# Filling idle TensorE time by a leaky bucket of owed columns instead of a trailing sum, in a transformer layer

## The chip, the cores and the metric

The kernel runs on one core of a Trainium2 chip. A core has five engines that matter here, each with its own instruction queue that it works off in order: TensorE (PE, with its weight loads shown apart as PEld), VectorE (DVE), ScalarE (ACT), GpSimd (POOL) and SyncE (SP), which only starts DMAs. The metric is device time in microseconds (us) from the start of an execution to its end. Three executions of the kernel before took 1261.03, 1268.29 and 1271.53 us, so the median is 1268.29. Such a time is one whole execution; the profile shows one more.

## The reference

One layer on 2048 tokens of width 512, all in bf16: a layer norm without scale, attention with 32 heads of 16, the output projection and a residual; then a second layer norm, a gated feed-forward part (GEGLU, width 1792) and a residual.

```python
qkv = layernorm(x) @ wqkv                      # 512 -> 3 * 512, 32 heads of 16
scores = einsum("bhqd,bhkd->bhqk", q, k) * 16 ** -0.5
o = einsum("bhqk,bhkd->bhqd", softmax(scores), v)
h = x + merge_heads(o) @ wo
n = layernorm(h)
out = h + (gelu(n @ w_gate) * (n @ w_up)) @ w_down
```

The scores are 32 x 2048 x 2048, and every one goes through an exponential on ACT. That is the largest piece of work.

## The kernel before, in words

**Tiles and units.** The queries are cut into four chunks of 512 (`c`), the heads into eight groups of four (`slot`). A unit is one chunk and one slot, 32 units in all. In a unit, `qk` goes over 16 key tiles of 128 and four heads: one tile is a matmul of 32 rows of the array (a head's 16 values beside another's, which the query mask sets to zero) with 512 query columns, into a PSUM bank of 128 x 512. Four such matmuls with different rows of the array can run side by side. `exps` takes the exponential of three or two banks at a time (the steps, in turn on banks 0 to 2 and 3 to 4; bank numbers are those of `SLOTS`) into the ring `PT`. `pv` multiplies four tiles of `PT` with the values: 17 columns a head (16 values and a column of ones for the softmax sum), four heads side by side in strips of the array's columns, summed over the 16 key tiles in bank `PVB`. After the 16th, `ofin` copies that bank out on DVE (L1340), transposes it on PE (L1344) and divides.

**Dense work.** Projections (at the start) and, per chunk, the output projection, the layer norm (`post`) and the feed-forward part (`gates`, `ups`, `downs`) are full-array matmuls into two further banks (`DENSE`, 6 and 7). They are laid into the time in which ACT works on the exponentials. The last chunk's follow behind the attention.

**What sets the order.** The order of every engine is set before the kernel runs, by a planner in Python (`Sched`). Each operation has a guessed duration (`TMM` 0.24 us for a matmul of 512 columns, `TQK` 0.34 for a step's score matmuls, `TPV` 0.33 for a value group, 0.093 + 0.427 us a tile for an exponential), the planner keeps a clock for each engine (`sch.t`) and picks the operation that can start first, with priorities (scores -10, values -5, dense work by due times). On the chip each engine then works its list off in that order and waits on semaphores; the guessed durations play no part any more.

**Fills.** Ahead of each PE operation that the planner is about to issue, `run` calls `fill(st)`, where `st` is the operation's planned start. A fill is a matmul of a 128 x 128 weight of zeros (`zero_bf`) with 512 columns of ones. It adds zero to `PVB` while a unit's sum is under way (L1511), and otherwise writes a free dense bank (L1521). `t0` is the time at which it could start; `st - t0` is the gap. If `fill` issues one, it is called again for the same operation. Each PE operation carries its column count, `cols`: 512 for a fill, 128 for each score matmul (a quarter of the array's rows), 512 for a value group, 512 for each dense matmul. `busy_columns` adds up the columns of the operations that ended in the last 3.4 us of planned time, and `fill` issues nothing where that sum is 3900 or more.

The matmuls of the profile stand under helper lines: L1144 is any dense matmul, L1145 any matmul with a place in the array, so the scores (`pbank<-QT,KT`) and the values (`pbank<-PT,VA`), L1151 any ACT operation made by `ACTF` (the exponentials).

Of the kernel before, what the change touches and what calls it, by code (L numbers as in the profile page):

```python
# [5 lines left out]
class _Eng:  # L6
    def __init__(self, name, sem):
        self.name = name
        self.sem = sem
        self.count = 0  # L10
        self.ops = []
        self.known = {}
        self.group_start = None
# [155 lines left out]
NT, NCH, NSLOT = 16, 4, 8  # L169
# [5 lines left out]
NT, NCH, NSLOT = 16, 4, 8  # L175
# [703 lines left out]
class Sched:  # L879
# [5 lines left out]
    def __init__(self, P, banks):  # L885
        self.P = P
        self.t = {n: 0.0 for n in P.ENGINES}
        self.done = {}
        self.streams = []
        self.banks = [(0.0, b) for b in banks]  # L890
        self.now = 0.0
        self.fill = None
        self.cols = []

    def add(self, gen, prio):
        s = Stream(gen, prio)
# [29 lines left out]
                    r = max(r, self.done[tok])  # L926
        return r + LAT

    def busy_columns(self, t):

        while self.cols and self.cols[0][0] < t - 3.4:
            self.cols.pop(0)
        return sum(n for _, n in self.cols)

    def _emit(self, op, start):
        if op.cols:
            self.cols.append((start + op.dur, op.cols))
        P = self.P
        extra = op.extra() if op.extra else ()
        for tok in extra:  # L940
            start = max(start, self.done[tok] + LAT)
        self.now = max(self.now, start)
        end = start + op.dur
        if op.dma is not None:
            tok = P.dma(op.eng, op.fns[0], op.dma, reads=op.reads, writes=op.writes, extra_deps=extra)
            self.t[op.eng] = start + 0.1
            self.done[tok] = end
        else:
            if op.eng == "pe":
                P.group_begin("pe")  # L950
            n = len(op.fns)
            for i, fn in enumerate(op.fns):
                tok = P.op(op.eng, fn, reads=op.reads, writes=op.writes, sig=(i == n - 1), extra_deps=extra)
            if op.eng == "pe":
                P.group_end("pe")
            self.t[op.eng] = end
            self.done[tok] = end
        if op.then is not None:
            op.then()
# [54 lines left out]
TMM, TTR, TTR32, TQK, TPV = 0.24, 0.12, 0.26, 0.34, 0.33  # L1014
SLOTS = ((0, 3), (3, 2))
PVB = 5
DENSE = (6, 7)
COLS = 3900


def bass_sequential_preLN__mha_block__geglu_ffn__prompt_kernel(nc, A_x, A_wqkv, A_wo, B_x, B_w_gate, B_w_up, B_w_down, out):
# [37 lines left out]
def fast_path(nc, P, base0, ARENA, pbank, flag, A_x, A_wqkv, A_wo, B_x, B_w_gate, B_w_up, B_w_down, out):  # L1059
# [67 lines left out]
    while sum(n for _, n, _ in STEPS) < len(TILES):  # L1127
        b0, n = SLOTS[len(STEPS) % len(SLOTS)]
# [6 lines left out]
    sch = Sched(P, list(DENSE))  # L1135
    C = dict(exp=0, pv=0, oa=0, ln1=0, proj=0, oproj=0, gut=0, down=0, act=0)
# [375 lines left out]

    def fill(st):

        if sch.t["pe"] < 10 or C["down"] >= 4 * NCH - 1:
            return False
        if C["pv"] % NT and C["pv"] < NT * NU:
            op = fill_op
        elif sch.banks:
            b = min(sch.banks)[1]  # L1520
            op = Op("pe", TMM, lambda e: e.matmul(pbank[:, b, :], zero_bf[:], ones_bf[:], start=True, stop=True), reads=["zero_bf", "ones_bf"], writes=[("pb", b)], cols=512)  # L1521
        else:
            return False
        t0 = max(sch.t["pe"], sch._ready(op))
        if st - t0 < TMM or sch.busy_columns(t0) >= COLS:
            return False
        sch._emit(op, t0)
        C["fill"] = C.get("fill", 0) + 1
        return True
# [58 lines left out]
```

## Time and profile before

| | before |
|---|---|
| median of three executions | 1268.29 us (1261.03 to 1271.53) |
| the profiled execution | 1261.9 us |
| its span, first to last instruction | 1260.1 us |
| mean granted TensorE clock | 0.708 |
| PE busy | 1138.9 us (90%), 5723 matmuls |
| ACT busy | 997.6 us (79%) |
| DVE, POOL busy | 259.5 us, 181.7 us |

In the page, the part with 40 slices gives each engine's busy share in tenths for each fortieth of the span (9 is 90% or more), and PEclk the share of full speed that TensorE's clock was granted. A busy PE is not PE at its peak: a matmul takes longer at a lower clock and is busy all that time. The windows view gives the same for stretches that one chooses, with the count of instructions in brackets; PEld counts weight loads, of which each matmul has one. In a row of groups or waits, what stands behind the bar or the arrow is the engine's idle time and what ended it. Some matmul records are missing in the trace: 386 fills of L1511 have a record and 435 of their weight loads.

### The profile page before, as it was taken

How to read it: one execution, taken by the hardware profiler on the slowest of the kernel's cores; microseconds unless marked ns; L12 is line 12 of the kernel's file. 1: busy time of each engine (PE TensorE's matmuls, PEld its weight loads, DVE VectorE, ACT ScalarE, POOL GpSimd, SP SyncE). 2: the span in 40 equal slices, each digit the busy share in tenths (PEclk: the TensorE clock that was granted, in tenths of full speed). 3: DMA queues.
4: the chain of work that ended last, by engine and by line, in shares of the span. 5: the costliest groups of instructions: out<-in, count | busy, mean ns of one | idle time of the engine just before them, and what ended most of it. 6: DMA issues, size and time to landing. Idle time of an engine off the chain costs nothing.

```text
span 1260.1 us, 14333 instructions
## 1 busy us (share of the span) xinstructions
PE 1138.9 (90%) x5723; PEld 276.7 (22%) x5827; DVE 259.5 (21%) x462; ACT 997.6 (79%) x897; POOL 181.7 (14%) x191
## 2 busy tenths in 40 slices
PE   7899999988998979989999999899989989999887
PEld 2222111111222221111222211111222221111132
DVE  5336100000355100000345100000056200000052
ACT  3799877777899997878889977777799997787610
POOL 6400000000076000000067000000058100000010
PEclk8899655555699995555689955555599985555599
DMA  4000500000000100000000000000000000000000
GB/s 133 1 1 1 192 1 1 1 1 1 1 2 1 35 1 1 1 1 1 1 1 1 25 10 1 1 1 1 1 1 2 9 26 1 1 1 1 1 1 20
DMA packets 12844, 14.91 MB, mean 12 GB/s; under 512 B 1760, under 2 KB 11744, under 8 KB 12768
## 3 DMA queue, kind: packets, MB, share of 16 engines
q1 hardware_dynamic: 12768, 13.90, 3.4%
q8 instruction: 48, 0.79, 0.3%
q14 instruction: 28, 0.23, 0.1%
HBM read 11.80 MB, written 2.10 MB: 11 GB/s over the span
## 4 chain that ended last, share of the span: by engine, by line
PE 72%; ACT 10%; POOL 7%; issue 6%; DVE 2%; ACTq 0%; DVEq 0%
PE pbank L1145 39%; PE pbank L1511 16%; PE pbank L1144 13%; ACT PT L1151 10%; POOL w_sb L1433 3%; PE pbank L1344 2%; POOL w_sb L1431 2%; POOL w_sb L1432 2%; DVE OA L1340 1%; POOL xn_sb L1220 1%; PE pbank L1521 1%; PE pbank L1381 0%; DVE g_sb L1429 0%; DVE QT L1268 0%; ACT w_sb L1439 0%
## 5 line engine op out<-in xcount | busy, mean ns | idle before, releaser
L1151 ACT ACTIVATE PT<-pbank 128x1536 bf16<-128x1536 f32 (+1 forms) x819 | 959.3, 1247 | 180.6 <-PE pbank L1145 177.0
L1145 PE MATMUL pbank<-QT,KT 32*128 32x512 bf16 x2048 | 420.7, 509 | 44.0 <-ACT PT L1151 39.0
L1145 PE MATMUL pbank<-PT,VA 128*17 128x512 bf16 x2048 | 264.3, 506 | 2.2 <-DVE OA L1340 1.0
L1511 PE MATMUL pbank<-ones_bf,zero_bf 128*128 128x512 bf16 x386 | 226.6, 587 | 36.5 <-PE pbank L1145 21.3
L1145 PEld LDWEIGHTS pbank<-QT,KT 32*128 32x128 bf16 x2048 | 83.3, 95 | 364.4 <-ACT PT L1151 160.7
L1340 DVE COPY OA<-pbank 128x512 f32<-128x512 f32 x32 | 22.1, 690 | 672.4 <-PE pbank L1145 672.4
L1397 POOL TENSOR_SCALAR rstd_95<-mv_94 128x1 f32<-128x1 f32 x16 | 3.6, 223 | 976.6 <-DVE mv_94 L1395 976.6
L1511 PEld LDWEIGHTS pbank<-ones_bf,zero_bf 128*128 128x128 bf16 x435 | 44.7, 103 | 216.4 <-PE pbank L1511 117.5
L1145 PEld LDWEIGHTS pbank<-PT,VA 128*17 128x17 bf16 x2048 | 50.4, 89 | 182.6 <-PE pbank L1511 68.9
L1144 PE MATMUL pbank<-wd_sb,GUT 128*128 128x512 bf16 x211 | 58.6, 382 | 3.2 <-PE pbank L1145 1.3
L1433 POOL TENSOR_TENSOR w_sb<-w_sb,g_sb 128x512 f32<-128x512 f32 x42 | 54.7, 1303 | 3.5
L1431 POOL TENSOR_TENSOR w_sb<-g_sb 128x512 f32<-128x512 f32 x42 | 47.9, 1141 | 31.6 <-DVE g_sb L1429 31.5
L1344 PE MATMUL pbank<-ident_77,OA 128*128 128x128 f32 x128 | 37.6, 388 | 4.5 <-DVE OA L1340 3.6
L1440 DVE SCALAR_TENSOR_TENSOR w_sb<-w_sb,g_sb 128x512 f32<-128x512 f32 x42 | 35.3, 840 | 18.9 <-ACT w_sb L1439 18.6
L1144 PE MATMUL pbank<-xnT,wqkv_sb 128*128 128x512 bf16 x121 | 36.9, 391 | 2.0 <-DVE xnT L1234 0.7
L1429 DVE COPY g_sb<-pbank 128x512 f32<-128x512 f32 x42 | 29.0, 690 | 40.2 <-PE pbank L1144 40.1
L1445 ACT ACTIVATE w_sb<-pbank 128x512 f32<-128x512 f32 x14 | 8.4, 597 | 35.8 <-PE pbank L1144 35.8
L1439 ACT ACTIVATE w_sb<-w_sb 128x512 f32<-128x512 f32 x42 | 26.7, 635 | 8.7 <-POOL w_sb L1433 8.7
L1432 POOL TENSOR_SCALAR w_sb<-w_sb 128x512 f32<-128x512 f32 x42 | 32.9, 784 | 3.7
L1465 DVE SCALAR_TENSOR_TENSOR GUT<-pbank,w_sb 128x512 bf16<-128x512 f32 x42 | 28.7, 688 | 19.7 <-PE pbank L1144 19.3
L1268 DVE TENSOR_SCALAR QT<-pbank,qmask 128x512 bf16<-128x512 f32 x31 | 23.3, 751 | 8.1 <-PE pbank L1144 6.8
L1220 POOL TENSOR_SCALAR xn_sb<-x_sb,mv,rstd 128x512 bf16<-128x512 bf16 x12 | 24.8, 2076 | 0.5 <-issue 0.3
(99 smaller groups left out, 470.9 us busy)
## 6 DMA issues: line engine op xcount, KB each, us to landing
xres<-in_A_x_dram SPq DMA_DIRECT2D x16, 128.0 KB, 3.3
out_dram<-out_sb SPq DMA_DIRECT2D x16, 128.0 KB, 1.7
wg_sb<-in_B_w_gate_dram SPq DMA_DIRECT2D x1, 1792.0 KB, 7.0
wu_sb<-in_B_w_up_dram SPq DMA_DIRECT2D x1, 1792.0 KB, 12.4
wd_sb<-in_B_w_down_dram SPq DMA_DIRECT2D x1, 1792.0 KB, 17.1
x_sb<-in_A_x_dram SPq DMA_DIRECT2D x3, 512.0 KB, 7.8
wqkv_sb<-in_A_wqkv_dram SPq DMA_DIRECT2D x2, 384.0 KB, 8.1
x_sb<-in_A_x_dram SPq DMA_DIRECT2D x2, 256.0 KB, 3.2
```

The costliest lines, as they stand in the source:

```text
L1144: return lambda e: e.matmul(o, l, r, start=start, stop=stop)
L1145: return lambda e: e.matmul(o, l, r, start=start, stop=stop, tile_position=tile)
L1151: return lambda e: e.activation(out=o, in_=i, func=func, **kw)
L1220: lambda e, t=t: e.tensor_scalar(out=xn_sb[:, t % 8, :], in0=x_sb[:, t, :], scalar1=mv[:, t, 0:1], scalar2=rstd[:, t:t + 1], op0=ALU.subtr ...
L1340: yield Op("dve", 0.61, lambda e: e.tensor_copy(out=OA[:, par, :], in_=pbank[:, PVB, :]), reads=[("pb", PVB)], writes=[("OA", par)])
L1344: yield Op("pe", 2 * TTR32, cols=256, fns=[lambda e, qt=qt: e.transpose(out=pbank[:, b, 128 * qt:128 * qt + 128], in_=OA[:, par, 128 * qt: ...
L1429: yield Op("dve", 0.61, lambda e: e.tensor_copy(out=gs, in_=pbank[:, b, :]), reads=[("pb", b)], writes=[("g", i)], extra=dE)
L1431: yield Op("pool", 1.05, lambda e: e.tensor_tensor(out=ws, in0=gs, in1=gs, op=ALU.mult), reads=[("g", i)], writes=[("w", i)])
L1432: yield Op("pool", 0.62, lambda e: e.tensor_scalar(out=ws, in0=ws, scalar1=GA, scalar2=1.0, op0=ALU.mult, op1=ALU.add), reads=[("w", i)], ...
L1433: yield Op("pool", 1.27, lambda e: e.tensor_tensor(out=ws, in0=ws, in1=gs, op=ALU.mult), reads=[("w", i), ("g", i)], writes=[("w", i)])
L1440: yield Op("dve", 0.6, lambda e: e.scalar_tensor_tensor(out=ws, in0=ws, scalar=1.0, in1=gs, op0=ALU.add, op1=ALU.mult), reads=[("w", i), ( ...
L1511: fill_op = Op("pe", TMM, lambda e: e.matmul(pbank[:, PVB, :], zero_bf[:], ones_bf[:], start=False, stop=False, skip_group_check=True), re ...
```

## The change

The trailing sum `busy_columns` goes, and `owed` takes its place: a number of columns that grows by 1250 with each microsecond of planned time, up to 1500, and from which each planned PE operation takes its columns at its planned end, down to zero and no further. A fill is now issued

- if 800 or more are owed, whatever the gap is, also where the gap is negative and the fill starts after the time at which the operation behind it could have;
- if 300 or more are owed and the gap is at least 0.06 us;
- if 100 or more are owed and the gap is at least `TMM`, 0.24 us.

Before, the gap had to be 0.24 us in all cases. The first fill may now come after the first score step is planned, where it was 10 us of PE's planned time. The fill itself, its banks and its end are as they were.

```diff
-        self.cols = []
+        self.debt = (0.0, 0.0)
...
-    def busy_columns(self, t):
-
-        while self.cols and self.cols[0][0] < t - 3.4:
-            self.cols.pop(0)
-        return sum(n for _, n in self.cols)
+    def owed(self, t, n=0):
+
+        d = min(1500.0, self.debt[1] + RATE * (t - self.debt[0]))
+        if n:
+            self.debt = (t, max(0.0, d - n))
+        return d

     def _emit(self, op, start):
         if op.cols:
-            self.cols.append((start + op.dur, op.cols))
+            self.owed(start + op.dur, op.cols)
...
-COLS = 3900
+RATE = 1250
+OWED = (100, 300, 800)
...
-        if sch.t["pe"] < 10 or C["down"] >= 4 * NCH - 1:
+        if "qk" not in C or C["down"] >= 4 * NCH - 1:
             return False
...
         t0 = max(sch.t["pe"], sch._ready(op))
-        if st - t0 < TMM or sch.busy_columns(t0) >= COLS:
+        n, gap = sch.owed(t0), st - t0
+        if n < OWED[0] or (gap < TMM and n < OWED[1]) or (gap < 0.06 and n < OWED[2]):
             return False
```

## The prediction

> **What bounds the kernel now.** I read the page first, for the clock over the span.
>
> ```profile
> span 1260.1 us, 14333 instructions
> ...
> PE   7899999988998979989999999899989989999887
> ...
> ACT  3799877777899997878889977777799997787610
> POOL 6400000000076000000067000000058100000010
> PEclk8899655555699995555689955555599985555599
> ```
>
> One slice is 31.5 us. The granted TensorE clock is full where projections or the feed-forward part run beside the attention, and half in four long stretches where the attention runs alone. PE shows nine tenths in both, so its busy share says nothing about the clock. ACT shows 9 at full clock and 7 at half. POOL's work, the feed-forward part's, starts in the slice after each of the three rises in the middle of the span. The windows view, cut at the changes of the clock, gives the sizes (columns: us, then the busy time and instruction count of PE, PEld, DVE, ACT and POOL, then the granted clock, DMA share, GB/s):
>
> ```profile
> 63.00:133.90 70.90, 67.49 (x444) 18.92 (x448) 37.72 (x56) 69.24 (x61) 0.00 (x0) 1.00 0.05 14
> 133.90:335.30 201.40, 184.53 (x797) 37.98 (x807) 8.84 (x20) 156.04 (x133) 0.00 (x0) 0.50 0.07 26
> 437.70:468.40 30.70, 23.78 (x163) 6.98 (x163) 1.38 (x3) 30.70 (x28) 0.00 (x0) 1.00 0.06 17
> 468.40:618.60 150.20, 138.15 (x599) 28.81 (x609) 6.77 (x15) 117.43 (x100) 0.00 (x0) 0.50 0.00 1
> 724.40:915.50 191.10, 175.80 (x755) 36.16 (x768) 9.29 (x20) 148.39 (x127) 0.00 (x0) 0.50 0.01 2
> 1028.20:1196.00 167.80, 153.12 (x652) 31.16 (x663) 6.19 (x13) 129.24 (x111) 0.00 (x0) 0.50 0.00 1
> 1196.00:1260.10 64.10, 52.92 (x225) 18.57 (x230) 24.57 (x48) 8.36 (x14) 3.16 (x8) 0.95 0.03 10
> ```
>
> At full clock the kernel is bound by ACT: its exponentials are busy 69.24 of 70.90 us (0.977) beside the projections, and 30.70 of 30.70 in the one stretch of attention alone that kept the clock. In the four half-clock stretches, 710.5 us together, ACT works 551.1 us (0.776) and waits for the score matmuls. The waits and the groups put this on the same lines:
>
> ```profile
> ACT PT L1151 <- PE pbank L1145: 177.0, 216, 7.0
> ...
> L1151 ACT ACTIVATE PT<-pbank 128x1536 bf16<-128x1536 f32 (+1 forms) x819 | 959.3, 1247 | 180.6 <-PE pbank L1145 177.0
> ```
>
> So 177 us of ACT's waiting is what is to be won, 159.4 us of it in those stretches (710.5 - 551.1).
>
> **What sets the clock.** The clock's changes lie on a grid of about 3.41 us, so I cut six such windows of attention alone at full clock and counted the weight loads in each (matmul records can be missing, so I count PEld). First line L1145, the scores and the value matmuls (each worth 128 columns of the whole array: 32 of 128 rows, or a 32-wide strip of columns), then L1511, the fills (512 columns each):
>
> ```profile
> 441.07:444.48 3.41, 1.43 (x16) 0.40 (x16) 1.00 0.00 0
> 451.31:454.72 3.41, 1.66 (x18) 0.48 (x15) 1.00 0.00 0
> 461.55:464.96 3.41, 1.26 (x13) 0.29 (x9) 1.00 0.00 0
> 464.96:468.38 3.42, 2.14 (x18) 0.63 (x18) 1.00 0.00 0
> 720.96:724.38 3.42, 1.82 (x15) 0.54 (x15) 1.00 0.32 93
> 1024.75:1028.16 3.41, 2.02 (x18) 0.54 (x15) 1.00 0.00 0
> ...
> 441.07:444.48 3.41, 0.62 (x2) 0.19 (x2) 1.00 0.00 0
> 451.31:454.72 3.41, 1.17 (x3) 0.38 (x4) 1.00 0.00 0
> 461.55:464.96 3.41, 1.07 (x3) 0.38 (x4) 1.00 0.00 0
> 464.96:468.38 3.42, 0.22 (x2) 0.10 (x1) 1.00 0.00 0
> 720.96:724.38 3.42, 0.36 (x1) 0.10 (x1) 1.00 0.32 93
> 1024.75:1028.16 3.41, 0.27 (x1) 0.10 (x1) 1.00 0.00 0
> ```
>
> The first three were followed by full clock: 16 x 128 + 2 x 512 = 3072 columns, 15 x 128 + 4 x 512 = 3968, 9 x 128 + 4 x 512 = 3200. The last three were each followed by the drop: 18 x 128 + 512 = 2816, 15 x 128 + 512 = 2432, and 2432 again. So I read the clock as kept by about 2900 columns in a window, and the fills as counting: without them 451.31 would stand at 1920 and should have dropped.
>
> **The change, part by part.** Before, a fill needed a gap of 0.24 us in the plan (TMM) and fewer than 3900 columns in the last 3.4 us. Now owed columns grow by 1250 per us up to 1500, each planned matmul pays its columns off, and a fill goes in at 800 owed whatever the gap (even ahead of a ready score matmul), at 300 if the gap is at least 0.06 us, and at 100 if it is 0.24. The bucket can't go below zero, so dense work earns no credit and owes again at once when it stops; the old sum went on holding the dense columns for 3.4 us.
>
> *Number of fills.* One pair of steps of the attention (a 3-tile and a 2-tile exponential) is 959.3 us / 409.5 = 2.34 us of ACT, and its matmuls are 5 x 128 + 5 x 128 = 1280 columns. At 1250 per us a pair of the plan's 2.32 us (2 x 0.093 + 5 x 0.427, the plan's constants) is owed 2900, so (2900 - 1280) / 512 = 3.16 fills a pair. Before:
>
> ```profile
> L1511 PEld LDWEIGHTS pbank<-ones_bf,zero_bf 128*128 128x128 bf16 x435 | 44.7, 103 | 216.4 <-PE pbank L1511 117.5 <-PE pbank L1145 96.0 <-issue 2.9
> ...
> 133.90:335.30 201.40, 59.49 (x98) 11.48 (x111) 0.50 0.07 26
> 437.70:468.40 30.70, 7.93 (x21) 2.30 (x24) 1.00 0.06 17
> 468.40:618.60 150.20, 44.71 (x74) 8.49 (x82) 0.50 0.00 1
> 724.40:915.50 191.10, 55.86 (x93) 10.87 (x105) 0.50 0.01 2
> 1028.20:1196.00 167.80, 52.90 (x88) 10.07 (x97) 0.50 0.00 1
> ```
>
> The half-clock stretches hold 111 + 82 + 105 + 97 = 395 fills on 551.1 / 2.34 = 235 pairs, 1.68 a pair; the stretch from 437.70 holds 24 on 13.1 pairs, 1.83. So about 1.4 fills a pair are new. A window of 3.41 us then holds 1250 x 3.41 = 4260 columns, 1350 above the reading of the bound. The worst place is the end of a unit, where PE waits for the copy of PVB: a hole of 1 us would take 1250 and leave 3000, still above the highest window that dropped (2816).
>
> *What they cost on PE at full clock.* The timeline of PE shows the spacing:
>
> ```profile
> 446.84 0.39 PE L1145 MATMUL pbank<-PT,VA 128*17 128x512 bf16 x4
> 447.43 0.39 PE L1145 MATMUL pbank<-QT,KT 32*128 32x512 bf16 x2 [0.20 <-ACT PT L1151]
> 447.75 1.29 PE L1511 MATMUL pbank<-ones_bf,zero_bf 128*128 128x512 bf16 x3
> 448.97 0.39 PE L1145 MATMUL pbank<-QT,KT 32*128 32x512 bf16 x3
> 449.30 0.39 PE L1145 MATMUL pbank<-PT,VA 128*17 128x512 bf16 x4
> ```
>
> A score or value group takes its place for 0.32 us (447.43 to 447.75), three fills in a row for 1.22 (447.75 to 448.97), 0.41 each, because a fill's weight load waits for the fill before it (117.5 us of the wait above); a fill alone I put at the 0.32 of any single group. A pair is then 2 score groups + 1.25 value groups at 0.32 = 1.04 us, and 3.16 fills at 0.32 to 0.41 = 1.01 to 1.30: PE 2.05 to 2.34 us against ACT's 2.34. From the other side: in the stretch from 437.70 PE idles 6.92 us on 13.1 pairs, 0.53 a pair, and 1.33 more fills take 0.43 to 0.55. So ACT stays the bound, but PE's slack is nearly spent, and PE works in order: a score group behind a forced fill comes late by what of the fill is not covered by ACT's other bank set. The nearest row for an almost full PE is 63.00 to 133.90, PE busy 67.49 of 70.90, ACT at 0.977. I take 0.96, a little under it, since the forced fill goes ahead of scores; 1.00 (the row from 437.70) and 0.93 are the ends. [...]
>
> *The sum.* 551.1 us of ACT at 0.96 takes 574 us in place of 710.5: 136 us gained (159 at 1.00, 118 at 0.93). The stretch that was warm already loses 1 us (30.7 / 0.96). Where dense work runs, the trace's windows are at full clock and there is little to gain; forced fills there and in the last 64.10 us, where nothing covers PE, are bounded by some ten fills of 0.41, 4 us lost, and by 3 us won where the tail now starts warm (the last stretch ends at half clock); I take zero. The planner's counter costs nothing on the chip. The profiled execution took 1261.9 us, 1.8 over its span and 6.4 under the median of 1268.29; from it, 1261.9 - 136 + 1 = 1127 us. With 1.00 and the tail's gain it is 1100, with 0.93 and the tail's loss 1150.
>
> **The rivals.** *PE takes ACT's place as the bound.* If most fills come in runs, or the plan's clipping at zero lets more than 3.16 in, PE needs more than 2.34 us a pair. At ACT 0.90 the stretches take 612 us, a gain of 98: 1164. For it speaks the arithmetic above, at its upper end; against it the row from 63.00, where PE carries denser work.
>
> *The clock drops in one stretch.* A window below about 2900, at a unit's end, and the clock stays at half until dense work comes, as it did four times before (in the page the first three stretches end just ahead of POOL's work). At half clock a fill in a run costs 0.62 us (300.45 to 302.32, three of them):
>
> ```profile
> 300.45 1.94 PE L1511 MATMUL pbank<-ones_bf,zero_bf 128*128 128x512 bf16 x3
> 302.32 0.61 PE L1145 MATMUL pbank<-QT,KT 32*128 32x512 bf16 x3
> ```
>
> Of 235 pairs each then has 1.48 fills more, 1.48 x 0.62 x 235 = 215 us, less at most the 58.9 us that PE idles there (710.5 - 651.6): 157 to 215 in all, some 46 a stretch, and its gain of 34 is gone: 1127 + 80 = 1207.
>
> *The columns do not hold the clock at all, and it is slower.* The place is the same four stretches, the price 157 to 215 us: 1419 to 1477, 1440 in the middle. It decides where a window with 4260 columns drops all the same. For it: zero weights might count for less than real data, and my bound rests on six windows. Against it: the window from 451.31. [...]
>
> *It does not do what it says.* If the plan has no room left, the fills stay near 435 and the time near 1262. Against it: PE's idle 0.53 us a pair in the warm stretch, much of it in gaps under 0.24 that are now open.
>
> **How the numbers follow.** The forecast has 0.68 (1100 to 1150), PE as the bound 0.10 (1150 to 1175), one lost stretch 0.07 (around 1207), no hold of the clock 0.10 (around 1440), no effect 0.05. The range from 1100 to 1175 holds the first two, 0.78. About 1% is what a measurement of this kernel can tell from no change: its three runs lie between 1261.03 and 1271.53. Faster by more is the first three, 0.85; the same 0.05; slower 0.10.
>
> **What would show it.** In the profile after, PEclk reads 8 or 9 in all slices after the first, with no run of 5s; L1511's weight loads go from 435 to 800 or 1000 (248 pairs of attention alone x 3.16 = 784, and some elsewhere); the mean of a score matmul falls from half-clock values to 0.39 us; ACT's wait for L1145 falls from 177 to 20 to 60 us. If PE is the bound, that wait stays near 80 at full clock. A half clock in slices with three fills a pair would prove the reading of the columns wrong, and fills near 435 the count.

## The result and the profile after

The changed kernel takes 1128.15 us (median of four executions, 1125.82 to 1130.49) against 1267.28 (median of four, 1261.03 to 1271.53). The ratio is 0.8906, with a 95% interval of 0.8864 to 0.8948. Its profiled execution took 1128.3 us over a span of 1126.6. The code moved down by two lines: scores and values are now L1147, exponentials L1153, fills L1513 (on `PVB`) and L1523.

The page of the changed kernel, the span and the rows of its 40 slices:

```profile
span 1126.6 us, 15044 instructions
...
PE   7899999898998998999899999899999998998887
...
ACT  3599999999999999999999999999999999999420
...
PEclk9799999999999999999999999999999999999999
```

The four runs of fives are gone. PE reads as before, so its busy share again tells nothing; ACT is at 9 from the third slice to the end of the attention. PEclk reads 7 in the second slice, because the full clock begins at 44.0 us here and at 38.3 us in the kernel before.

The windows view of the changed kernel, with the columns as in the prediction:

```profile
63.00:133.90 70.90, 68.34 (x440) 18.78 (x446) 34.80 (x52) 69.04 (x61) 0.00 (x0) 1.00 0.00 1
133.90:300.00 166.10, 150.06 (x917) 44.20 (x933) 13.03 (x27) 157.21 (x137) 0.00 (x0) 1.00 0.11 37
...
410.00:580.00 170.00, 153.49 (x961) 46.11 (x976) 20.12 (x44) 162.27 (x143) 6.11 (x11) 1.00 0.01 3
...
1062.00:1126.00 64.00, 52.70 (x212) 17.31 (x216) 22.30 (x42) 8.36 (x14) 3.17 (x8) 0.97 0.03 10
```

Where the attention runs almost alone (10 and 24 weight loads of dense matmuls in the second and third row) ACT is busy 0.946 (157.21 / 166.1) and 0.955 of the time, at a granted clock of 1.00. It was 0.776 at 0.50. The rows for the stretch from 63 us and for the last 64 us are nearly as they were, so the gain lies between them, in the attention.

The groups of the changed kernel:

```profile
L1153 ACT ACTIVATE PT<-pbank 128x1536 bf16<-128x1536 f32 (+1 forms) x819 | 949.4, 1245 | 55.4 <-PE pbank L1147 52.0
L1147 PE MATMUL pbank<-QT,KT 32*128 32x512 bf16 x2048 | 316.5, 385 | 19.5 <-ACT PT L1153 9.9
L1513 PE MATMUL pbank<-ones_bf,zero_bf 128*128 128x512 bf16 x707 | 275.4, 389 | 48.4 <-PE pbank L1147 15.3
...
L1513 PEld LDWEIGHTS pbank<-ones_bf,zero_bf 128*128 128x128 bf16 x776 | 74.4, 96 | 246.5 <-PE pbank L1513 141.9
```

ACT's wait for scores fell from 177.0 to 52.0 us, and the weight loads of the fills rose from 435 to 776.

### The profile page after: what moved, and what is told of

Read it like the earlier page. It is cut to its first block, busy times and chain, and to the rows that moved or that the text cites. A ratio compares the mean times of both kernels' runs of the same rounds, so it can differ in the third digit from the quotient of the medians.

```text
span 1126.6 us, 15044 instructions
## 1 busy us (share of the span) xinstructions
PE 1017.5 (90%) x6105; PEld 298.4 (26%) x6220; DVE 257.5 (23%) x462; ACT 987.4 (88%) x897; POOL 181.0 (16%) x191
## 4 chain that ended last, share of the span: by engine, by line
PE 76%; POOL 8%; issue 6%; ACT 5%; DVE 2%; POOLq 0%; ACTq 0%; DVEq 0%
PE pbank L1147 34%; PE pbank L1513 23%; PE pbank L1146 15%; ACT PT L1153 5%; POOL w_sb L1435 3%; POOL w_sb L1433 2%; POOL w_sb L1434 2%; PE pbank L1523 2%; PE pbank L1346 2%; POOL xn_sb L1222 1%; DVE OA L1342 1%; DVE g_sb L1431 0%; PE pbank L1405 0%; PE pbank L1383 0%; DVE VA L1282 0%
## 5 line engine op out<-in xcount | busy, mean ns | idle before, releaser
L1153 ACT ACTIVATE PT<-pbank 128x1536 bf16<-128x1536 f32 (+1 forms) x819 | 949.4, 1245 | 55.4 <-PE pbank L1147 52.0
L1147 PE MATMUL pbank<-QT,KT 32*128 32x512 bf16 x2048 | 316.5, 385 | 19.5 <-ACT PT L1153 9.9
L1513 PE MATMUL pbank<-ones_bf,zero_bf 128*128 128x512 bf16 x707 | 275.4, 389 | 48.4 <-PE pbank L1147 15.3
L1147 PE MATMUL pbank<-PT,VA 128*17 128x512 bf16 x2048 | 202.1, 385 | 4.1 <-PE pbank L1147 0.8
L1147 PEld LDWEIGHTS pbank<-QT,KT 32*128 32x128 bf16 x2048 | 77.7, 91 | 240.2 <-issue 139.7
L1513 PEld LDWEIGHTS pbank<-ones_bf,zero_bf 128*128 128x128 bf16 x776 | 74.4, 96 | 246.5 <-PE pbank L1513 141.9
L1147 PEld LDWEIGHTS pbank<-PT,VA 128*17 128x17 bf16 x2048 | 49.7, 87 | 124.4 <-PE pbank L1513 59.0
L1346 PE MATMUL pbank<-ident_77,OA 128*128 128x128 f32 x128 | 27.9, 300 | 2.3 <-DVE OA L1342 2.1
L1523 PE MATMUL pbank<-ones_bf,zero_bf 128*128 128x512 bf16 x69 | 26.9, 393 | 2.5 <-DVE GUT L1467 1.0
```

Source lines behind the costliest of these rows:

```text
L1147: return lambda e: e.matmul(o, l, r, start=start, stop=stop, tile_position=tile)
L1153: return lambda e: e.activation(out=o, in_=i, func=func, **kw)
L1346: yield Op("pe", 2 * TTR32, cols=256, fns=[lambda e, qt=qt: e.transpose(out=pbank[:, b, 128 * qt:128 * qt + 128], in_=OA[:, par, 128 * qt: ...
L1513: fill_op = Op("pe", TMM, lambda e: e.matmul(pbank[:, PVB, :], zero_bf[:], ones_bf[:], start=False, stop=False, skip_group_check=True), re ...
```

## The experiments

My theory was that the clock is held by how many columns of the whole array are worked in each few microseconds, and that the fills supply them. The rivals: the clock follows PE's busy time (the share of time in matmuls); the bucket's even spacing counts and not the number; the short gaps and the forced fills are what holds it.

**Fills a quarter as large.** The order and the number of fills stay. The fill that writes a dense bank (L1523) is edited in the same way.

```diff
-matmul(pbank[:, PVB, :], zero_bf[:], ones_bf[:], ...)
+matmul(pbank[:, PVB, :], zero_bf[0:32, :], ones_bf[0:32, :], ..., tile_position=(0, 0))
```

> The changed kernel with the same order and the same 849 fills, but each fill uses 32 of the array's 128 rows (512 columns in the same PE time, a quarter of the array). If the clock is held by columns of the whole array, a unit of attention alone has 16,896 + 41 x 128 columns in some 30.5 us, about 2480 in a window of 3.41 us, under the 2816 that dropped: half clock in the four stretches, and 1380 to 1480 us, since the fills still take their time. If it is held by the time that PE is busy, the same full clock as with whole fills and 1125 to 1132 us.

It took 1384.98 us (one execution). The page of this run, the busy time and PEclk:

```profile
PE 1297.5 (94%) x6220; PEld 282.7 (20%) x6220; DVE 257.9 (19%) x462; ACT 1007.8 (73%) x897; POOL 180.7 (13%) x191
...
PEclk9999555555599955555599955555599955555579
```

PE is busy 94% of the span, more than the 90% of the changed kernel, and the clock is at half in the same four stretches as before the change. Nothing but the part of the array that a fill uses was changed. A matmul takes longer at half clock (a score group 0.61 us at 302.32 in the kernel before, against 0.39 at 448.97 at full clock), so the windows that count most are those at full clock just ahead of a drop. The windows view of the first three of them in this run:

```profile
138.60:142.01 3.41, 3.11 (x18) 0.79 (x15) 0.00 (x0) 3.41 (x4) 0.00 (x0) 1.00 1.03 413
425.30:428.70 3.40, 3.14 (x22) 0.87 (x20) 1.31 (x3) 3.40 (x4) 0.72 (x1) 1.00 0.02 5
476.50:479.90 3.40, 3.05 (x22) 0.83 (x18) 0.00 (x0) 3.40 (x4) 0.00 (x0) 1.00 0.62 185
```

PE is busy 0.90 to 0.92 in them, and the clock dropped all the same. So PE's busy time didn't hold the clock here. The area of the array that the fills work is all that differs from the changed kernel, and the mean granted clock is 0.676 in place of 0.992. The test changed the rows that a fill uses; that a value matmul, with its strip of columns, counts as 128 is no experiment of its own.

**The old sum without its gap rule.**

```diff
-        if st - t0 < TMM or sch.busy_columns(t0) >= COLS:
+        if sch.busy_columns(t0) >= COLS:
```

> The kernel before with its trailing sum of 3900 columns, but without the rule that a gap must be 0.24 us: 802 fills, 33 to 43 in a unit of attention alone (before 456 and 21 to 26; changed kernel 849 and 37 to 43). If the number of fills counts and the gap rule kept it low, the clock holds and it takes 1124 to 1136 us. If the even spacing by the bucket counts, stretches drop to half clock and it takes 1180 us or more.

It took 1485.53 us (1467.27 to 1488.97), ratio 1.1807 (1.1705 to 1.191): slower than before, with almost as many fills as the changed kernel (802 against 849). The timeline of PE in this run, just before the clock's drop at 528 us (the line numbers are those of the kernel before):

```profile
522.10 0.39 PE L1521 MATMUL pbank<-ones_bf,zero_bf 128*128 128x512 bf16 x1
522.42 0.39 PE L1145 MATMUL pbank<-PT,VA 128*17 128x512 bf16 x4
522.74 0.44 PE L1344 MATMUL pbank<-ident,OA 128*128 128x128 f32 x2
523.11 0.39 PE L1145 MATMUL pbank<-QT,KT 32*128 32x512 bf16 x3
523.43 0.40 PE L1145 MATMUL pbank<-PT,VA 128*17 128x512 bf16 x4
523.99 0.39 PE L1145 MATMUL pbank<-QT,KT 32*128 32x512 bf16 x2 [0.16 <-ACT PT L1151]
524.31 0.40 PE L1145 MATMUL pbank<-PT,VA 128*17 128x512 bf16 x4
525.33 0.39 PE L1145 MATMUL pbank<-QT,KT 32*128 32x512 bf16 x3 [0.63 <-ACT PT L1151]
525.66 2.84 PE L1511 MATMUL pbank<-ones_bf,zero_bf 128*128 128x512 bf16 x6
528.43 1.03 PE L1145 MATMUL pbank<-QT,KT 32*128 32x512 bf16 x5
```

Without the gap rule the sum issues fills until it is full, six in a row here, and then none until columns are 3.4 us old. Ahead of them stand over 3 us without a fill (from 522.49 to 525.66), and the scores at 528.43 come 2.8 us after the six began. The window of 3.41 us that ends at the drop holds 3 weight loads of scores and 5 of fills, 2944 columns. So this order has the fills, but not in each window. Once at half clock, the many fills keep PE full: it is busy 110.36 of 120 us, 54.20 of them in fills. The windows view of this run in a half-clock stretch, then its fills alone:

```profile
150.00:270.00 120.00, 110.36 (x401) 20.29 (x399) 2.75 (x6) 71.19 (x61) 0.00 (x0) 0.50 0.00 1
...
150.00:270.00 120.00, 54.20 (x90) 9.35 (x90) 0.50 0.00 1
```

**The same with a short memory.** A sum over 1.2 us and 1450 columns, also without the gap rule.

```diff
-        while self.cols and self.cols[0][0] < t - 3.4:
+        while self.cols and self.cols[0][0] < t - 1.2:
...
-COLS = 3900
+COLS = 1450
...
-        if st - t0 < TMM or sch.busy_columns(t0) >= COLS:
+        if sch.busy_columns(t0) >= COLS:
```

> The kernel before with the gap rule left out, as in the run of 1486 us, but with a trailing sum over 1.2 us and 1450 columns in place of 3.4 us and 3900: 31 to 36 fills in a unit of attention alone. If the long memory laid the fills in bursts of six with holes between, and the holes lost the clock, the short memory holds it: 1090 to 1130 us. If any trailing sum without the gap rule loses it, stretches are at half clock: 1330 to 1480 us.

Four executions took 1091.66, 1121.43, 1179.94 and 1182.2 us. The profiled one (1182.2) was at half clock in one of the four stretches alone. Its page:

```profile
PEclk9899855555555799999999999999999999999889
```

So most of the 1486 us went with the long memory; this order also has somewhat fewer fills (31 to 36 a unit against 33 to 43), so the two are not told apart. The short memory didn't hold the clock every time: in the order given, the mean clocks of the four executions are 0.990, 0.952, 0.884 and 0.880. In the profile the stretch was lost at 135.93 us, where the projections stop: the window ahead holds 5 weight loads of scores, 2 of transposes and 3 of fills, 2432 columns. Why the execution of 1091.66 us kept the clock isn't settled.

**The bucket with the old gap rule.** Nothing forced, no gap under 0.24 us.

```diff
-OWED = (100, 300, 800)
+OWED = (100, 10 ** 9, 10 ** 9)
```

> The changed kernel with the old gap rule: a fill needs 100 owed and a gap of 0.24 us, nothing is forced and no short gap is used: 738 fills, 33 to 38 in a unit of attention alone, about 3980 columns in a window. If the count per window decides, the clock holds, and with fewer fills ahead of scores ACT is busier (0.96 to 0.98): 1115 to 1128 us. If the fills in short gaps are what holds the clock, it drops in some stretch: 1160 to 1270 us.

1092.93 us (1091.92 to 1094.79), ratio 0.8691 (0.8615 to 0.8767), which is faster than the changed kernel. The clock held from 38 us to the end; the mean clocks of the four executions are 0.993 to 0.995. So in these four executions neither the forced fills nor those in short gaps were needed, and the kernel without them is 35 us faster.

**The old sum with a higher limit.** All else as before.

```diff
-COLS = 3900
+COLS = 4800
```

> The kernel before with its trailing sum at 4800 columns in place of 3900, and its gap of 0.24 us: 33 to 37 fills in a unit of attention alone, the same as the full-gap bucket, which took 1093 us. If the number of fills is what the change bought, the clock holds here too: 1088 to 1098 us. If the sum's memory of dense columns leaves a hole where the dense work stops, the clock drops there and, once dropped, 36 fills a unit keep PE too full: 1330 to 1480 us.

1096.19 us (1093.54 to 1097.37), ratio 0.8668 (0.8617 to 0.8718), the same within 4 us as the bucket with the same gap rule. Its profile has one drop, of 3.4 us at 855 us. The change in kind, from a sum to a bucket, is not what brought the gain: the number of fills is. Two rules together had kept it low. With the gap rule and a limit of 4800 there are 33 to 37 fills a unit, and with the limit of 3900 and no gap rule 33 to 43, where the kernel before has 21 to 26. But the number alone isn't enough: the two sums without a gap rule had about as many and lost the clock, the long one in every execution, the short one in three of four.

**What the 35 us are.** First the forced fills alone are taken out:

```diff
-OWED = (100, 300, 800)
+OWED = (100, 300, 10 ** 9)
```

> The changed kernel without the fills that go in at 800 owed whatever the gap; those in gaps of 0.06 us at 300 owed stay: 825 fills (changed kernel 849, the full-gap kernel 738). The full-gap kernel took 1093 us and the changed one 1128, both at full clock; this splits the 35 us. If the forced fills ahead of ready scores cost it: 1093 to 1105 us. If the fills in short gaps do: 1120 to 1130 us. If it is the number of fills alone, 24 of 111 fills less give about 1120 us.

1118.09 us (1117.2 to 1118.78), ratio 0.8839 (0.8787 to 0.889): near what the number of fills alone gave, 1120. Then the rate is set to 1100, with the old gap rule and, without the second line of this diff, with the three rules of the change:

```diff
-RATE = 1250
+RATE = 1100
-OWED = (100, 300, 800)
+OWED = (100, 10 ** 9, 10 ** 9)
```

> The changed kernel with 1100 owed columns per us and the gap of 0.24 us for every fill: 29 to 33 in a unit of attention alone, about 3680 columns in a window. At 1000 per us with the short gaps two of five runs lost the clock in a stretch (1118 and 1128 us against 1079 to 1083). With 240 columns more in a window I expect the clock to hold in every run: 1080 to 1090 us, none over 1100. If the holes at the ends of units rather than the mean decide, some runs still lose a stretch: over 1110 us.

> The changed kernel with 1100 owed columns per us and its own three gap rules: 29 to 33 fills in a unit of attention alone, the same as the kernel with 1100 and the full gap, which took 1079 us. If it is the number of fills that fills PE and costs the 35 us between the changed kernel and the full-gap one, this takes 1078 to 1088 us too. If fills in short gaps and forced fills cost by where they stand, it takes 1095 to 1115 us.

With the old gap rule 1079.32 us (1075.09 to 1080.87), ratio 0.8532 (0.8495 to 0.857); with the three rules 1080.11 (1078.82 to 1085.37). At the same number of fills the rules make no difference to the time. The two orders do differ: the planner forces 108 of the 641 fills of the second and lays 99 into short gaps. So the number costs, not the place. The windows view shows how, for 120 us of attention; the second row of each counts the fills alone. The changed kernel:

```profile
170.00:290.00 120.00, 108.06 (x652) 31.41 (x661) 4.54 (x10) 113.86 (x99) 0.00 (x0) 1.00 0.00 1
...
170.00:290.00 120.00, 53.77 (x138) 14.37 (x150) 1.00 0.00 1
```

The bucket with the old gap rule at 1250:

```profile
170.00:290.00 120.00, 112.10 (x688) 31.73 (x684) 9.97 (x23) 117.93 (x104) 1.04 (x3) 1.00 0.00 1
...
170.00:290.00 120.00, 49.87 (x128) 12.25 (x128) 1.00 0.00 1
```

The same at 1100:

```profile
170.00:290.00 120.00, 106.13 (x687) 31.38 (x701) 13.30 (x30) 119.88 (x107) 2.41 (x6) 1.00 0.00 1
...
170.00:290.00 120.00, 38.10 (x98) 10.34 (x109) 1.00 0.00 1
```

With 150, 128 and 109 fills ACT is busy 0.949, 0.983 and 0.999 of the time, at the same clock. The last 6 and 10 us of the second and third stretch already hold dense matmuls (from 284.2 and 280.1 us). From 170 to 270 us none of these kernels has any, and six orders compare as follows, by the same view:

| order | weight loads of fills in 100 us | ACT busy, us |
|---|---|---|
| the changed kernel | 124 | 94.77 |
| without forced fills | 123 | 95.02 |
| old gap rule, 1250 | 117 | 98.24 |
| old sum at 4800 | 116 | 98.23 |
| old gap rule, 1100 | 104 | 100.00 |
| three rules, 1100 | 100 | 99.90 |

Orders with nearly the same number of fills have the same share, whichever rule laid them. Against the old gap rule at 1100, the changed kernel has 776 - 590 = 186 more weight loads on L1513 and takes 48.8 us longer, 0.26 us a fill; the old gap rule at 1250 has 99 more and takes 13.6 us longer, 0.14 a fill. The price rises with the number. That this is PE's slack running out is the reading; PE's busy time can't rank all six, since some matmul records are missing in four of them. The two with all fills recorded in these 100 us agree with it: PE is busy 93.42 us under the old gap rule at 1250 and 89.75 under the three rules at 1100.

**Fewer fills.** At 1000 columns per us, with the three rules:

```diff
-RATE = 1250
+RATE = 1000
```

> The changed kernel with 1000 owed columns per us in place of 1250: 557 fills, 27 to 29 in a unit of attention alone, about 3440 columns in a window of 3.41 us. If about 2900 columns hold the clock, it holds with PE less full, ACT at 0.975: 1110 to 1122 us. If the bound is higher or single windows fall under it, a stretch drops: 1150 to 1260 us.

Of five executions three took 1079.17 to 1083.47 us and two 1117.73 and 1127.73. The profiled one is the last, and its page shows why:

```profile
PEclk9899999999999999999999975555589999999989
```

One of the four stretches, 164 us of it, was at half clock. At 850:

```diff
-RATE = 1250
+RATE = 850
```

> The changed kernel with 850 owed columns per us: 399 fills, 19 to 20 in a unit of attention alone, fewer than the kernel before has (456 and 22 to 24), but evenly laid: about 3040 columns in a window of 3.41 us, with single windows some 500 lower. If each window must have about 2900, most stretches drop to half clock: 1210 to 1265 us. If even spacing and no hole after dense work is what counts, the clock holds and the time is 1070 to 1082 us.

1201.78 us (1198.85 to 1202.37), ratio 0.9495 (0.9439 to 0.9551), at half clock in all four stretches:

```profile
PEclk9899855555799995555699965555599985555589
```

So an even 19 to 20 fills a unit didn't hold the clock in any of four executions (mean clocks 0.722 to 0.732), 27 to 29 held it in three of five (0.987 to 0.993, against 0.920 and 0.935), and 29 to 33 held it in all ten executions of the two kernels at 1100, with mean clocks of 0.987 to 0.996. The kernel at 850 was still faster than the kernel before, at the same half clock. The windows view of 120 us of it, then its fills:

```profile
150.00:270.00 120.00, 112.85 (x505) 23.12 (x511) 4.54 (x10) 103.42 (x87) 0.00 (x0) 0.50 0.00 1
...
150.00:270.00 120.00, 33.39 (x55) 6.67 (x63) 0.50 0.00 1
```

And of the kernel before:

```profile
150.00:270.00 120.00, 110.25 (x474) 22.33 (x480) 4.12 (x9) 93.95 (x81) 0.00 (x0) 0.50 0.00 1
...
150.00:270.00 120.00, 37.04 (x61) 7.26 (x70) 0.50 0.00 1
```

ACT is busy 103.42 us with 63 fills and 93.95 with 70; in the run of 1486 us above it was 71.19 with 90. In time per pair of exponentials, the three rows have 1.45, 1.73 and 2.95 fills and take 2.76, 2.96 and 3.93 us. In these three orders, the fills that didn't hold the clock were pure cost.

## Why the prediction was right, point by point

**What bounds the kernel.** ACT's exponentials at full clock, the score matmuls at half, where ACT was busy 0.776 of the time: shown. With the clock held and PE not too full, ACT is busy 0.999 of the time (the run at 1100).

**What sets the clock.** The step that carried the forecast, that fills count by their area and about 4260 columns in a window hold the clock, is shown by the quarter fills and by the runs from 850 to 1250; by its weight loads the changed kernel has some 4170 columns to a window between 133.9 and 300 us, all at full clock. The figure of 2900 columns as the bound of a single window was too sharp. A window is one step of the clock's changes: the kernel before's drops at 468.38, 724.38 and 1028.16 us lie 75 and 89 steps of 3.413 us apart. I counted all 2668 windows of 3.41 us at full clock in the twelve profiles the same way, from weight loads (128 for a transpose, 512 for a dense matmul, 128 for a quarter fill), between 60 us after the start and 70 us before the end, with the grid 0.1 us earlier. All 25 drops came after windows of 3072 columns or fewer, but 71 other windows of 3200 or fewer were passed, down to 2432. So in these runs no window of over 3200 was followed by a drop; at 3200 or fewer, 25 windows were and 71 weren't. That fits the kernel at 1000 (3440 on the average), which lost a stretch in two of five executions. The figure hangs on the grid: with the grid unshifted, one of the 25 windows ahead of a drop holds 3456.

Columns tell the two kinds of window apart far better than PE's busy time does: 45 passed windows hold no more columns than the fullest dropped one, while 1146 passed windows have PE less busy than the busiest dropped one (0.92). And the zero weights of the fills do count: at nothing in this sum, they would leave 1227 passed windows under the fullest dropped one in place of 45. With 512 for a value matmul in place of 128 it would be 1786.

The short gaps and the forced fills, which the mean doesn't need, raise the lowest window: it holds 3456 columns in the changed kernel against 2944 with the old gap rule at 1250, and 3328 against 2688 at 1100. So the old gap rule held the clock with windows that others dropped at, and there luck may have a part.

Of the signs that I named, one failed: PEclk reads 7 in the second slice. The mean of a score matmul, 385 ns, and ACT's wait, 52.0 us, came as forecast.

**Number of fills.** Forecast 3.16 a pair; the stretch from 170 has 150 fills on 99 / 2 = 49.5 pairs, 3.03. L1513's 776 loads are a little under the 800 to 1000 I gave, and near the 784 worked out for attention alone.

**Their cost.** ACT's share was 0.946 to 0.955 where I took 0.96. I laid the loss on forced fills standing ahead of ready scores. That reason fell: in the table above 124 fills with forced ones among them and 123 without give the same share, and so do the two runs at 1100. What the share follows is the number of fills. The bounds of PE's time a pair, 2.05 to 2.34 us, did say that PE's slack was nearly spent.

**The size of ACT's work.** The term that was mis-sized is 551.1 us for the half-clock stretches and 2.34 us a pair. It came from a time in which ACT waited often. At full pace a pair takes 120 / (107 / 2) = 2.24 us, since successive exponentials overlap (1302 ns each on the mean in that run, but 935.4 / 819 = 1.142 us of busy time). The 235 pairs of those stretches then take 526 us, the gain is 184, and the 1.00 end of the sum becomes 1261.9 - 184 = 1078 us in place of 1100. The run at 1100 with the old gap rule took 1079. In the changed kernel the smaller work (949.4 us busy against 959.3) and the smaller share nearly cancel, which is why 1127 and 1128 agree so closely; that closeness is partly luck.

**The rivals.** For losing the clock everywhere the price was 1419 to 1477 us (the middle is 1448, not 1440). The nearest run, the changed order with quarter fills, took 1385, under that price; the old sum without the gap rule took 1467 to 1489 with fills in bursts. One lost stretch cost the kernel at 1000 some 45 us (1127.7 - 1083), where I gave 80 for the changed kernel with its 40 fills a unit. That the clock follows PE's busy time, taken as the time in matmuls, doesn't agree with the quarter fills, whose PE is busy 94% of the span at a mean clock of 0.676. Against the rival that the change does nothing I argued with gaps under 0.24 us; the sum at 4800, with the old gap rule, shows that this was the wrong ground: gaps of 0.24 us were there for 33 to 37 fills a unit, once the limit was raised.

## What to carry to other kernels

Where TensorE's clock falls although it looks busy, count columns of the whole array in windows of a few microseconds beside its busy time. In this kernel's twelve profiles all 25 drops came after windows of 3.41 us with 3072 columns or fewer, and PE was busy up to 0.92 in them. Fill up to a little over what is seen to hold the clock, evenly enough that no window falls far under the mean. Then take away fills until some execution loses the clock: here 1100 owed columns per us (1079 us) beat 1250 (1128 us) and 1000 (1079, but 1118 to 1128 in two of five). A limit on fills needs several executions to judge, and fills that didn't hold the clock made this kernel slower: 1486 us with 802 of them in bursts, against 1268 with 456.

## What the runs showed that was not expected

The groups of the kernel at 1100 with the old gap rule:

```profile
L1153 ACT ACTIVATE PT<-pbank 128x1536 bf16<-128x1536 f32 (+1 forms) x819 | 935.4, 1302 | 20.0 <-PE pbank L1147 18.2
```

The same 819 exponentials keep ACT busy 935.4 us here, 949.4 in the changed kernel and 959.3 in the kernel before, while the mean of one grows from 1247 to 1302 ns: instructions that follow each other without a wait overlap (819 times 1302 ns is 1066 us, in 935.4 us of busy time). ACT's busy time, read where it waited often (180.6 us, in the kernel before), was thus too large a bound for what it took at full pace.

The start of the full clock differs between profiles: by the trace's clock it stayed up from 38.3 us in the kernel before and from 44.0 in the changed one, with nearly the same order ahead of it, and ACT had worked 33.47 us by 63 us in the one and 31.28 in the other. Whether the order or the execution makes this, one profile of each doesn't show. And no lowest count that holds the clock came out as a fixed number: the kernel at 1000 held it in three executions and lost it in two, with the same instructions.
